# Attention and two MoE layers on one core: v, k and q laid out for their loads, and the second product of the dense MLP in tiles of 384 tokens, every second one accumulated in PSUM onto a copy by ScalarE

## The chip, the cores and the metric

The kernel runs on one core of a Trainium2 chip. The metric is the device time of one execution in microseconds (us); less is better. The engines are PE (TensorE, matrix products), DVE (VectorE), ACT (ScalarE), POOL (GpSimd) and SP (SyncE, which issues the DMAs). PE writes its products to PSUM, which has eight banks; DVE and ACT read them from there.

## The reference

Three layers, one after the other, all in float32:

```python
p_packed = sm_attn(p, k, v)          # 4 batches, 8 heads, 32 packed queries, 576 keys, head size 64
x = sm_attn(q, p_packed, p_packed)   # 576 queries per batch -> x is [2304, 512]
h = x @ w_in                         # [512, 2048]
x = (h * (1.0 / (1.0 + np.exp(-h)))) @ w_out          # [2048, 512]: the dense MLP
P = exp(logits - max); 8 rounds of row and column normalisation   # gate, 8 experts
out = sum over e of P[:, e] * (max(x @ w1[e], 0) @ w2[e])
```

## The kernel before

Every float32 product is made of three products of reduced parts: an operand is split into a part `h` (a cast by ACT) and the rest `l` (a subtraction by DVE), and hh, hl and lh are added up in PSUM.

**Attention and chunk 0.** The tokens are 4 batches of 576. Their steps are small nodes of a planner (`plan`), which is given costs (for example 1.68 us on SP for a load of k), priorities (`PR`) and an order of loads (`LOADS`), and writes out the order of every engine ahead of time. Loads come as k and q in pieces of [128, 2, 576], v in [128, 4, 256] and [64, 256], and weights of the dense MLP, which arrive as 64-bit floats and are converted in some steps on ACT and DVE (`ctin`, `ctout`, then `win`, or `woh` and `wol`). In a batch PE makes scores `s` in two halves, DVE transposes them (`e`), sums and divides, transposes back to `a2f`, splits into `a2h` and `a2l`. From these gemm1 starts.

**The dense MLP.** The 2048 hidden columns are four chunks `c` of 512. The work of a chunk is in units of one half batch (288 tokens): `u` (the input weights times the packed values, split as `U`, or `Uh` and `Ul`), gemm1 (`g` at L633, four tiles of 12 matmuls of 128x288), the gate function (`graw` at L663, on ACT), its split into `gT` (L664 on ACT, L665 on DVE), and gemm2 (`g` at L686: 4 tiles of 128 output columns, 12 matmuls of 288 each). In chunk 0 ACT copies the tile to `x2a` (batches 0 and 1) or `x2b` (2 and 3) (L691), in chunks 1 to 3 DVE adds it to that (L693). gemm2 of a unit is put behind gemm1 of the next. Chunk 0 is the planner's; chunks 1 to 3 are an order written out by hand, in which `pump` after each tile takes a share `RATE[c]` of a step of `pre`, the weight forms of the second MoE.

**The second MoE's weight forms.** Sums and differences `S` of weight blocks are made by DVE (L807); each is cast to `po` by ACT (L144), its rest follows by DVE (L145), and SP stores both to device memory (`w1d<-po`). The pool `po` has two buffers. In chunk 3, once `gh` is opened at batch `order[c][2]`, all remaining forms are taken this way.

**The second MoE.** A first expert runs in plain form (`u` L1002, `d` L1021) while the forms `xg` of x are made; then seven products of blocks (`X`, `Y`, `Z` at L1157; `d` at L1109), in which some tiles of PSUM are first filled by an ACT copy (L1105), added to by PE, and copied back (L1117).

Of the kernel before, what the change touches and what calls it, by code (L numbers as in the profile page):

```python
# [28 lines left out]
RATE = {1: 42 / 64, 2: 37 / 64, 3: 35 / 42}  # L29
CONV = 0.55  # L30
# [19 lines left out]
}  # L50

LOADS = "o0 i3 i0 k0 o2 k3 i2 v0 i1 q0 k1 v3 v1 o1 q3 o3 g v2 q1 q2 k2"
# [52 lines left out]
def fused_kernel(  # L105
# [24 lines left out]
    hp, hp_st = pool("hp", 4, side="left")  # L130
# [28 lines left out]
    class Plan:  # L159
# [13 lines left out]
        def order(self):  # L173
# [6 lines left out]
            while left:  # L180
# [46 lines left out]
                for c, k in t["give"]:  # L227
# [7 lines left out]
                 "a1T": 2, "ppm": 2, "ct": 4, "one": 1, "y": 4, "cr": 2, "cc": 2})  # L235
    kv, a2, u, gT = {}, {}, {}, {}
    win, wout = {}, {}
# [20 lines left out]
    def plan_loads():  # L258
        def kq(n, b, g):
            def fn():  # L260
                t = att.tile([128, 2, S], F32, tag="kq", bufs=8, name=f"{n}{b}{g}")
                src = kT if n == "k" else qT
                fixed(nc.sync.dma_start(t, src[b, 256 * g:256 * g + 256, :]
                                        .rearrange("(j p) s -> p j s", p=128)))
                kv[n, b, g] = t
            plan.add((n, b, g), "SP", 1.68, fn, take=[("kq", 1)])

        def vv(b, g):
            def fn():
# [236 lines left out]
    def conv2(c, kind, j):  # L506
# [9 lines left out]
        z = cvp["t2"].tile([128, 1024], F32, tag="ct2", name=f"ct{kind}{c}{j}")  # L516
# [58 lines left out]
    def plan_conv1(kind):  # L575
        for j in range(2):
# [5 lines left out]
            plan.add(g + (1,), "ACT", 2.35, nx, [g + (0,)], take=[("cc", 1)])  # L582
            plan.add(g + (2,), "DVE", 1.42, nx, [g + (1,)])
            plan.add(g + (3,), "DVE", 1.25, nx, [g + (2,)])
            done = [("cr", 1)] + [("cc", 1)] * (kind == "in")
            plan.add(g + (4,), "DVE", 1.25, nx, [g + (3,)], take=[("w", 1)] if kind == "in" else [], give=done)
            if kind == "out":
                plan.add(g + (5,), "ACT", 1.08, nx, [g + (4,)], take=[("w", 2)])
                plan.add(g + (6,), "DVE", 1.25, nx, [g + (5,)], give=[("cc", 1)])
# [47 lines left out]
    def gemm1_tile(c, b, half, f):  # L637
# [18 lines left out]
    def gemm1(c, b, half, pump):  # L656
        for j in range(WID[c] // 256):
# [6 lines left out]
            act.copy(out=t[:, 0], in_=raw)  # L664
            dve.tensor_tensor(t[:, 1], raw, t[:, 0].bitcast(F32), op=ALU.subtract)  # L665
            for i in range(2):
                gT[c, b, half, 2 * j + i] = t[:, :, i]
# [515 lines left out]
    def sinkhorn():  # L1183
        lgs = {}
        for hh in (1, 0):
# [8 lines left out]
            lg = const.tile([32 * nj, w], F32, name=f"lgs{hh}")  # L1194
# [63 lines left out]
    def close_att():  # L1258
# [36 lines left out]
    pre = pre_w1(list(range(G0)), 0)  # L1295
# [8 lines left out]
    def pump_conv(w):  # L1304
        due[1] += w * CONV
        if due[1] >= 1:
            due[1] -= 1
            cvn.step()

    with tc.manual_schedule(engines={mybir.EngineType.PE, mybir.EngineType.DVE, mybir.EngineType.Activation}):  # L1310
        for i, (c, b) in enumerate(seq):
# [14 lines left out]
            for half in range(2):  # L1326
                if c == NC - 1 and b == order[c][0] and half == 0:
                    box["ct_st"].close()
                    cv_st.close()
# [7 lines left out]
                if half == 1 and nxt is not None:  # L1337
# [3 lines left out]
                if pend is not None:  # L1341
# [159 lines left out]
```

## Time and profile before

| | |
|---|---|
| median of 3 runs (lowest to highest) | 1790.02 us (1788.94 to 1791.48) |
| the profiled execution | 1790.24 us |
| its span, first to last instruction | 1788.5 us |
| PE busy | 1768.5 us, 99% |
| DVE busy | 1454.3 us, 81% |
| ACT busy | 1040.2 us, 58% |

The span is 1.7 us shorter than the execution's time. Busy shares are means over the whole span, and stages differ; a matmul's own duration overlaps with the next one's, so that the pace of PE is read from a stretch of many. The table does not tell what PE waits for; the rows further below do.

### The profile page before, as it was taken

How to read it: one execution, taken by the hardware profiler on the slowest of the kernel's cores; microseconds unless marked ns; L12 is line 12 of the kernel's file. 1: busy time of each engine (PE TensorE's matmuls, PEld its weight loads, DVE VectorE, ACT ScalarE, POOL GpSimd, SP SyncE). 2: the span in 40 equal slices, each digit the busy share in tenths (PEclk: the TensorE clock that was granted, in tenths of full speed). 3: DMA queues.
4: the chain of work that ended last, by engine and by line, in shares of the span. 5: the costliest groups of instructions: out<-in, count | busy, mean ns of one | idle time of the engine just before them, and what ended most of it. 6: DMA issues, size and time to landing. Idle time of an engine off the chain costs nothing.

```text
span 1788.5 us, 25903 instructions
## 1 busy us (share of the span) xinstructions
PE 1768.5 (99%) x9852; PEld 1510.3 (84%) x9852; DVE 1454.3 (81%) x1972; ACT 1040.2 (58%) x1631; POOL 1.0 (0%) x8
## 2 busy tenths in 40 slices
PE   6999999999999999999999999999999999999998
PEld 4999999999998888888888888888888888888887
DVE  7868897658776998999888999887777777777778
ACT  6766655445454566666666666656555555555555
POOL 0000000000000000000000000000000000000000
PEclk9999999999999999999999999999999999999999
DMA  9425866865665655455554555965455444545442
GB/s 338 176 95 208 298 236 255 305 210 175 212 212 171 216 197 168 174 188 192 197 171 167 176 171 200 323 234 165 153 168 165 163 153 143 169 159 169 150 130 94
DMA packets 146619, 341.78 MB, mean 191 GB/s; under 512 B 11952, under 2 KB 53568, under 8 KB 145600
## 3 DMA queue, kind: packets, MB, share of 16 engines
q1 hardware_dynamic: 146496, 340.14, 56.3%
q8 instruction: 77, 1.26, 0.3%
q14 instruction: 46, 0.38, 0.1%
HBM read 256.66 MB, written 83.44 MB: 190 GB/s over the span
## 4 chain that ended last, share of the span: by engine, by line
PE 94%; DMA 3%; DVE 2%; ACT 1%; issue 0%; SPq 0%; DVEq 0%; ACTq 0%
PE d L1109 33%; PE X L1157 19%; PE g L686 10%; PE Z L1157 10%; PE u L1002 5%; PE g L633 5%; PE Y L1157 5%; PE d L1021 5%; DMA v<-in_v_dram 1%; PE u L247 1%; DMA w1d<-po 1%; DMA rawout<-in_moe_w_out_dram 0%; DMA rawin<-in_moe_w_in_dram 0%; PE s L247 0%; PE lg L1191 0%
## 5 line engine op out<-in xcount | busy, mean ns | idle before, releaser
L145 DVE TENSOR_TENSOR lo<-hb,hi 128x1024 fp32r<-128x1024 f32 x224 | 273.7, 1222 | 33.2 <-ACT hi L144 32.2
L1109 PE MATMUL d<-hi,w2f 128*128 128x512 f32 x896 | 294.2, 389 | 0.0
L1157 PE MATMUL X<-xf,w1l 128*128 128x512 f32 x1152 | 276.9, 389 | 0.0
L144 ACT CAST hi<-hb 128x1024 fp32r<-128x1024 f32 x224 | 235.3, 1051 | 64.9 <-PE d L1109 59.5
L1157 PEld LDWEIGHTS X<-xf,w1l 128*128 128x128 f32 x1152 | 216.2, 188 | 44.9
L1121 DVE TENSOR_TENSOR M<-d,M 128x512 f32<-128x512 f32 x204 | 140.4, 688 | 100.7 <-PE d L1109 100.7
L1117 ACT COPY M<-d 128x512 f32<-128x512 f32 x234 | 137.4, 589 | 143.2 <-PE d L1109 140.2
L686 PE MATMUL g<-gT,woh 128*128 128x288 f32 x1024 | 207.4, 297 | 0.0
L1109 PEld LDWEIGHTS d<-hi,w2f 128*128 128x128 f32 x896 | 168.1, 188 | 35.0
L1109 PE MATMUL d<-lo,w2f 128*128 128x512 f32 x448 | 174.3, 389 | 0.0
L686 PEld LDWEIGHTS g<-gT,woh 128*128 128x128 f32 x1024 | 163.7, 188 | 12.3 <-issue 4.7
L1109 PE MATMUL d<-hi,w2l 128*128 128x512 f32 x512 | 167.8, 389 | 0.0
L686 PE MATMUL g<-gT,wol 128*128 128x288 f32 x512 | 150.5, 294 | 0.0
L1105 ACT COPY d<-M 128x512 f32<-128x512 f32 x216 | 127.1, 589 | 20.7 <-DVE M L1121 19.3
L1109 PE MATMUL d<-hi,w2g 128*128 128x512 f32 x384 | 125.7, 389 | 0.0
L1109 PEld LDWEIGHTS d<-hi,w2l 128*128 128x128 f32 x512 | 96.1, 188 | 20.3 <-ACT d L1105 0.4
L1164 ACT COPY cp<-X 128x512 f32<-128x512 f32 x128 | 74.5, 583 | 46.5 <-PE X L1157 46.4
L1109 PE MATMUL d<-lo,w2l 128*128 128x512 f32 x256 | 99.6, 389 | 0.0
L1109 PEld LDWEIGHTS d<-lo,w2f 128*128 128x128 f32 x448 | 84.1, 188 | 17.5
L1157 PE MATMUL Y<-xf,w1f 128*128 128x512 f32 x384 | 97.3, 389 | 0.0
L686 PEld LDWEIGHTS g<-gT,wol 128*128 128x128 f32 x512 | 96.4, 188 | 0.0
L1002 PE MATMUL u<-xs,w1h 128*128 128x256 f32 x512 | 94.4, 285 | 0.0
(205 smaller groups left out, 3317.1 us busy)
## 6 DMA issues: line engine op xcount, KB each, us to landing
r<-in_moe_w_dram SPq DMA_DIRECT2D x128, 512.0 KB, 4.1
w1l<-w1d SPq DMA_DIRECT2D x128, 512.0 KB, 4.0
w1d<-po SPq DMA_DIRECT2D x64, 512.0 KB, 4.4
w2d<-w2f SPq DMA_DIRECT2D x64, 512.0 KB, 4.1
w2l<-w2d SPq DMA_DIRECT2D x64, 512.0 KB, 3.7
rb<-in_moe_w_dram SPq DMA_DIRECT2D x96, 256.0 KB, 2.7
sb<-in_moe_w_dram SPq DMA_DIRECT2D x48, 256.0 KB, 2.8
pb<-pd SPq DMA_DIRECT2D x16, 512.0 KB, 5.2
```

The source lines that it names most:

```text
L144: act.copy(out=hi, in_=raw)
L145: eng.tensor_tensor(out=lo, in0=raw, in1=hi.bitcast(F32), op=ALU.subtract)
L633: pe.matmul(ps, lhs[:, fs], rhs, start=(n == 0), stop=(n == 5))
L686: pe.matmul(ps[:, :HS], lhs, rhs, start=(n == 0), stop=(n == 3 * nf - 1))
L1002: pe.matmul(ps[:, i], w[:, k % 2, f], x[:, k], start=(n == 0), stop=(n == 11))
L1021: pe.matmul(ps, h[:, l, f % 2, 128 * tt:128 * tt + 128], w[:, f % 2], start=(fh == 0 and n == 0), stop=(fh == 1 and n == 11))
L1105: act.copy(out=ps, in_=m)
L1109: pe.matmul(ps, w[:, l, c, 128 * d:128 * d + 128], r[:, c], start=(n == 0 and not seed), stop=(n == 5), skip_group_check=seed)
L1117: act.copy(out=m, in_=ps)
L1121: dve.tensor_tensor(m, ps, m, op=ALU.add)
L1157: pe.matmul(ps, w[:, l, c, 128 * i:128 * i + 128], x[:, r, c], start=(n == 0 and p in (1, 7)), stop=(n == 5), skip_group_check=p in (2, 6, ...
L1164: act.copy(out=t, in_=ps)
```

## The change

The host lays v, k and q out so that each load is contiguous per partition: a row of k or q is 4608 B in place of two of 2304 B, one of v 4 KB in place of four of 1 KB. The planner has new priorities, a new order of loads and new costs for them; the batches are now taken in the order 0, 2, 1, 3 (before 0, 3, 1, 2). The split gate values go to two rings that hold four half batches, so that gemm2 in chunks 1 to 3 can take tiles of 384 tokens (`gemm2_wide`, L725). From the ninth tile on each tile with an even `d` is seeded: ACT copies the slice of x2 to PSUM one tile ahead (`seed`, L710), PE adds the 12 products to it, ACT copies it back (L730). Odd tiles are added by DVE as before (L732). The buffers `ct2` of the conversion go, the values are converted in place; the forms `xg` begin at step 8 in place of 9. In the changed kernel the lines have other numbers: graw and its cast are L672 and L673, po L145, u L251, gemm1 L641.

```diff
-RATE = {1: 42 / 64, 2: 37 / 64, 3: 35 / 42}
-CONV = 0.55
+RATE = {1: 46 / 64, 2: 38 / 64, 3: 36 / 53}
+CONV = 0.6
+TW = 384
...
-LOADS = "o0 i3 i0 k0 o2 k3 i2 v0 i1 q0 k1 v3 v1 o1 q3 o3 g v2 q1 q2 k2"
+LOADS = "i2 o3 k0 o2 i0 k2 i1 v0 i3 q0 k1 v2 v1 q2 o0 g o1 k3 q1 q3 v3"
...
-                fixed(nc.sync.dma_start(t, src[b, 256 * g:256 * g + 256, :]
-                                        .rearrange("(j p) s -> p j s", p=128)))
+                fixed(nc.sync.dma_start(t, src[b, g]))
...
-            plan.add((n, b, g), "SP", 1.68, fn, take=[("kq", 1)])
+            plan.add((n, b, g), "SP", 1.52, fn, take=[("kq", 1)])
...
-            t = hp.tile([128, 2, 2, HS], F32R, tag="h", name=f"gT{j}")
+            q = (b % 2) * S + half * HS
+            hi, lo = (ring[j].rearrange("p (f l) s -> p l f s", l=2)[:, l, :, q:q + HS] for l in range(2))
...
-    def gemm2(c, b, half, psp, tag, pump):
-        for d in range(4):
-            for _ in gemm2_tile(c, b, half, d, psp, tag):
-                pass
-            pump(1.6)
+    seeded, wides = {}, [0]
+
+    def seed(c, sb, t, d):
+        if d % 2 == 0 and wides[0] >= 8:
+            k = (c, sb, t, d)
+            wides[0] += 1
+            seeded[k] = box["p3"].tile([128, 512], F32, tag="y", name=f"g2w{c}{sb}{t}{d}")
+            act.copy(out=seeded[k][:, :TW], in_=x2[sb][d][:, TW * t:TW * t + TW])
+
+    def gemm2_wide(c, sb, t, d, ahead, pump):
+        ps = seeded.pop((c, sb, t, d), None)
+        on = ps is not None
+        if not on:
+            wides[0] += 1
+            ps = box["p3"].tile([128, 512], F32, tag="y", name=f"g2w{c}{sb}{t}{d}")
+        if ahead:
+            seed(*ahead)
+        ds, q = slice(128 * d, 128 * d + 128), slice(TW * t, TW * t + TW)
+        n = 0
+        for f in range(4):
+            hi, lo = wout[c, f // 2]
+            for lhs, rhs in ((hi, 0), (hi, 1), (lo, 0)):
+                pe.matmul(ps[:, :TW], lhs[:, f % 2, ds], ring[f // 2][:, 2 * (f % 2) + rhs, q],
+                          start=(n == 0 and not on), stop=(n == 11), skip_group_check=on)
+                n += 1
+        dst = x2[sb][d][:, q]
+        if on:
+            act.copy(out=dst, in_=ps[:, :TW])
+        else:
+            dve.tensor_tensor(dst, ps[:, :TW], dst, op=ALU.add)
+        pump(2 + 2 / 15)
...
+                if unit_:
+                    tiles += [(c, b // 2, unit_ - 1, d) for d in range(4)]
+                keep = {0: 2, 1: 2, 2: 2, 3: 4}[unit_]
...
+                while len(tiles) > keep:
+                    n = tiles.pop(0)
+                    gemm2_wide(*n, tiles[0] if tiles else None, pump)
...
-                if s >= 9 and slot:
+                if s >= 8 and slot:
                     next(xg, None)
```

**ACT in the third quarter of chunk 3.** The rows are ACT's own order; `g1_3010` is gemm1 of chunk 3, batch 0, second half, first pair of tiles, `g2w3122` is the wide tile of chunk 3, x2b, t = 2, d = 2, and po14 and po15 are weight forms. Before:

```order
L663 ACTIVATE graw_4281<-g1_3001_4267 128x576
L664 CAST gT1_4280<-graw_4281 128x576
L144 CAST po14_6_4299<-S14_2_4228 128x512
L144 CAST po14_7_4318<-S14_3_4259 128x512
L144 CAST po14_5_4337<-S14_1_4226 128x512
L144 CAST po14_3_4356<-S14_4_4261 128x512
L663 ACTIVATE graw_4379<-g1_3010_4365 128x576
L664 CAST gT0_4378<-graw_4379 128x576
L663 ACTIVATE graw_4397<-g1_3011_4383 128x576
```

And now:

```order
L730 COPY x2b0_1366<-g2w3120_3887 128x384
L145 CAST po14_6_3968<-S14_2_3884 128x512
L145 CAST po14_7_3973<-S14_3_3902 128x512
L710 COPY g2w3122_3979<-x2b2_1368 128x384
L145 CAST po14_5_3994<-S14_1_3882 128x512
L672 ACTIVATE graw_4012<-g1_3010_3999 128x576
L673 CAST ring0_103<-graw_4012 128x2x288
L145 CAST po14_3_4016<-S14_4_3904 128x512
L672 ACTIVATE graw_4034<-g1_3011_4021 128x576
L673 CAST ring1_1742<-graw_4034 128x2x288
```

Before, four po casts stood in one piece ahead of graw; now a copy back stands ahead of them, a seed between the second and the third, and graw of `g1_3010` between the third and the fourth.

**DVE where the first batch's attention ends.** The rows are DVE's order; `a2l0` is the lower part of batch 0, which gemm1 reads, `ctout` are steps of the conversion of an output weight, `e_2<-s2_20` is the transposition of the scores of batch 2. Before:

```order
L496 ISA ctout01_613<-rawout01_374,ctout01_613 128x1024
L455 TENSOR_TENSOR a2l0_622<-a2f0_564,a2h0_621 128x1152
L608 TENSOR_TENSOR U030_640<-u030_627,U030_640 128x512
L608 TENSOR_TENSOR U031_657<-u031_628,U031_657 128x512
L504 TENSOR_TENSOR wol00_181<-ctout01_613,woh00_180 128x512
L483 TENSOR_SCALAR ctout03_672<-ctout03_672 128x512
L484 TENSOR_SCALAR ctout03_672<-ctout03_672 128x512
L485 SCALAR_TENSOR_TENSOR ctout03_672<-rawout03_389,ctout03_672 128x512
L496 ISA ctout03_672<-rawout03_389,ctout03_672 128x1024
L397 STREAM_TRANSPOSE e_3_725<-s2_30_648 128x576
```

And now:

```order
L461 TENSOR_TENSOR a2l0_636<-a2f0_569,a2h0_635 128x1152
L489 TENSOR_SCALAR ctout00_642<-ctout00_642 128x512
L490 TENSOR_SCALAR ctout00_642<-ctout00_642 128x512
L491 SCALAR_TENSOR_TENSOR ctout00_642<-rawout00_374,ctout00_642 128x512
L502 ISA ctout00_642<-rawout00_374,ctout00_642 128x1024
L489 TENSOR_SCALAR ctout01_646<-ctout01_646 128x512
L490 TENSOR_SCALAR ctout01_646<-ctout01_646 128x512
L491 SCALAR_TENSOR_TENSOR ctout01_646<-rawout01_393,ctout01_646 128x512
L502 ISA ctout01_646<-rawout01_393,ctout01_646 128x1024
L510 TENSOR_TENSOR wol00_690<-ctout00_642,woh00_689 128x512
L403 STREAM_TRANSPOSE e_2_712<-s2_20_571 128x576
```

Before, one conversion of an output weight stood ahead of `a2l0` and one between it and the transposition; now both stand behind `a2l0` and ahead of the transposition.

## Rows read from the trace of the kernel before

**Rows 1.** The page's table of engines, and the clock in 40 slices.

```profile
PE 1768.5 (99%) x9852; PEld 1510.3 (84%) x9852; DVE 1454.3 (81%) x1972; ACT 1040.2 (58%) x1631; POOL 1.0 (0%) x8
...
PEclk9999999999999999999999999999999999999999
```

**Rows 2.** PE's waits: engine line, what for, total us, times, longest.

```profile
PE u L247 <- ACT graw L663: 0.8, 1, 0.8
PE d L1021 <- DVE w2l L145: 0.8, 1, 0.8
```

**Rows 3.** Windows: us, busy (instructions) of PE, PEld, DVE, ACT, POOL, PEclk, DMA share, GB/s.

```profile
24.00:26.60 2.60, 2.21 (x19) 1.09 (x16) 2.40 (x5) 2.12 (x8) 0.00 (x0) 1.00 1.05 391
29.90:33.60 3.70, 3.16 (x57) 2.18 (x56) 3.67 (x6) 1.95 (x4) 0.00 (x0) 1.00 1.11 315
...
144.20:375.00 230.80, 229.90 (x1794) 219.60 (x1792) 193.66 (x318) 124.64 (x191) 0.00 (x0) 1.00 0.75 271
```

**Rows 4.** The chain that ended last: start us, us, what.

```profile
249.90 6.40 PE g L686 x48
...
456.78 2.87 PE u L1002 x24
...
564.53 2.72 PE X L1157 x12
```

**Rows 5.** Groups by line, 144.2 to 375 us: shapes, count, busy us, mean ns.

```profile
L144 ACT CAST po<-S 128x512 fp32r<-128x512 f32 x63 | 36.1, 619 | 24.0 <-DMA w1d<-po 16.6 <-DVE S L807 7.3
L664 ACT CAST gT<-graw 128x576 fp32r<-128x576 f32 x44 | 29.7, 675 | 1.4
L663 ACT ACTIVATE graw<-g 128x576 f32<-128x576 f32 x44 | 28.6, 650 | 65.3 <-PE g L633 65.2
...
L145 DVE TENSOR_TENSOR po<-S,po 128x512 fp32r<-128x512 f32 x64 | 43.4, 684 | 9.7 <-ACT po L144 9.7
...
L693 DVE TENSOR_TENSOR x2b<-g,x2b 128x288 f32<-128x288 f32 x48 | 21.6, 452 | 3.7 <-PE g L686 3.5
```

**Rows 6.** The page's costliest groups: the copy that fills a PSUM tile.

```profile
L1105 ACT COPY d<-M 128x512 f32<-128x512 f32 x216 | 127.1, 589 | 20.7 <-DVE M L1121 19.3
```

**Rows 7.** Groups by line on ACT, 44 to 144 us.

```profile
L691 ACT COPY x2b<-g 128x288 f32<-128x288 f32 x16 | 6.0, 404 | 8.9 <-PE g L686 8.9
```

**Rows 8.** DVE's timeline, 26.5 to 52 us: start, us, instruction, idle before.

```profile
27.39 1.45 DVE L397 STREAM_TRANSPOSE e<-s 128x576 f32<-128x576 f32 x2 [0.51 <-PE s L247]
...
39.20 0.43 DVE L483 TENSOR_SCALAR ctout<-ctout 128x512 f32<-128x512 f32 x1 [0.24 <-ACT ctout L480]
...
41.56 1.35 DVE L455 TENSOR_TENSOR a2l<-a2f,a2h 128x1152 fp32r<-128x1152 f32 x1
42.83 1.28 DVE L608 TENSOR_TENSOR U<-u,U 128x512 fp32r<-128x512 f32 x2
```

**Rows 9.** PE's timeline, 40 to 53 us.

```profile
43.15 0.80 PE L633 MATMUL g<-a2h,U 128*128 128x288 f32 x4
...
50.66 1.25 PE L247 MATMUL u<-win,ppT 64*32 64x512 f32 x16
51.84 0.53 PE L686 MATMUL g<-gT,woh 128*128 128x288 f32 x2
```

**Rows 10.** ACT's timeline, 331 to 354 us.

```profile
332.83 1.13 ACT L144 CAST po<-S 128x512 fp32r<-128x512 f32 x2
339.44 0.62 ACT L144 CAST po<-S 128x512 fp32r<-128x512 f32 x1 [5.48 <-DMA w1d<-po]
...
353.61 0.62 ACT L144 CAST po<-S 128x512 fp32r<-128x512 f32 x1 [7.67 <-DMA w1d<-po]
```

**Rows 11.** The page's DMA issues: KB each, median us from issue to landing.

```profile
w1d<-po SPq DMA_DIRECT2D x64, 512.0 KB, 4.4
```

**Rows 12.** DVE's timeline, 552 to 560 us.

```profile
557.74 2.36 DVE L145 TENSOR_TENSOR w2l<-r,w2h 128x1024 fp32r<-128x1024 f32 x2
```

More of the change, by code (lines that the diff above doesn't have):

```diff
@@ L234, in fused_kernel @@
     plan = Plan({"p": 4, "s": 2, "kq": 8, "vt": 4, "w": 14, "x": 4, "h": 4, "g": 2, "a1": 2,
-                 "a1T": 2, "ppm": 2, "ct": 4, "one": 1, "y": 4, "cr": 2, "cc": 2})
+                 "a1T": 2, "ppm": 2, "ct": 4, "one": 1, "y": 4, "cr": 2})
     kv, a2, u, gT = {}, {}, {}, {}
+    ring = [hp.tile([128, 4, 2 * S], F32R, tag="h0", name="ring0")]
+    kq4 = hp.tile([128, 4, 2, S], F32, tag="h1", name="kq4")
+    kqn = []
     win, wout = {}, {}
@@ L515, in conv2 @@
         low, high = words[:, :, 0], words[:, :, 1]
-        z = cvp["t2"].tile([128, 1024], F32, tag="ct2", name=f"ct{kind}{c}{j}")
+        if kind == "in":
+            win[c, j] = unit([128, 2, w], F32, f"win{c}{j}")
+            z = win[c, j].rearrange("p k f -> p (k f)")
+        else:
+            z = unit([128, 1024], F32, f"ct{c}{j}")
         zi = z.bitcast(U32)
@@ L581, in plan_conv1 @@
             plan.add(g + (0,), "SP", 3.0, nx, ["close"], take=[("cr", 1)])
[L582 removed]
+            plan.add(g + (1,), "ACT", 2.35, nx, [g + (0,)], take=[("w", 1)])
             plan.add(g + (2,), "DVE", 1.42, nx, [g + (1,)])
             plan.add(g + (3,), "DVE", 1.25, nx, [g + (2,)])
[L585 to L586 removed]
+            plan.add(g + (4,), "DVE", 1.25, nx, [g + (3,)], give=[("cr", 1)])
             if kind == "out":
                 plan.add(g + (5,), "ACT", 1.08, nx, [g + (4,)], take=[("w", 2)])
[L589 removed]
+                plan.add(g + (6,), "DVE", 1.25, nx, [g + (5,)], give=[("w", 1)])
     up_ps = {}
@@ L643, in gemm1_tile @@
             gpair[k] = gt.tile([128, 2, HS], F32, tag="graw", name="graw")
-            hpair[k] = hp.tile([128, 2, 2, HS], F32R, tag="h", name=f"gT{f}")
-        raw, t = gpair[k], hpair[k]
+            hpair[k] = ring[0][:, len(hpair) % 4].rearrange("p (i l s) -> p i l s", i=2, l=2)
+        raw, t = gpair[k], hpair[k].rearrange("p i l s -> p l i s")
         act.activation(raw[:, i], ps[:, :HS], AF.Silu)
@@ L660, in gemm1 @@
                 gemm1_mm(ps[:, i, :HS], c, b, half, 2 * j + i)
-            t = hp.tile([128, 2, 2, HS], F32R, tag="h", name=f"gT{j}")
+            q = (b % 2) * S + half * HS
+            hi, lo = (ring[j].rearrange("p (f l) s -> p l f s", l=2)[:, l, :, q:q + HS] for l in range(2))
             raw = gt.tile([128, 2, HS], F32, tag="graw", name="graw")
             act.activation(raw, ps[:, :, :HS], AF.Silu)
[L664 to L667, printed above, removed]
+            act.copy(out=hi, in_=raw)
+            dve.tensor_tensor(lo, raw, hi.bitcast(F32), op=ALU.subtract)
             pump(0.8)
@@ L1265, in close_att @@
             open_(name, n, keep=name in ("S", "r1"))
+        box["pre"] = pre_w1(list(range(G0)), 0)
+        next(box["pre"])
         cvp["p2"], box["cv_st"] = pool("cv2", 2, side="right", reuse_waits="tile")
-        cvp["t2"], box["ct_st"] = pool("ct2", 2, side="right", reuse_waits="tile")
         cv1.update({(1, kind, j): conv2(1, kind, j) for kind in ("in", "out") for j in range(2)})
@@ L1294, in fused_kernel @@
     cvn = None
-    pre = pre_w1(list(range(G0)), 0)
+    pre = box["pre"]
+    next(pre)
+    next(pre)
     due = [0.0, 0.0]
@@ L1308, in pump_conv @@
             cvn.step()
+    tiles = []
+    ring.append(hp.tile([128, 4, 2 * S], F32R, tag="h1", name="ring1"))
     with tc.manual_schedule(engines={mybir.EngineType.PE, mybir.EngineType.DVE, mybir.EngineType.Activation}):
@@ L1336, in fused_kernel @@
                 gemm1(c, b, half, pump)
-                if half == 1 and nxt is not None:
+                if nxt is not None and half == ((c, b) != seq[NC][:2]):
                     if nxt[0] != c:
@@ L1340, in fused_kernel @@
                     make_u(*nxt)
-                if pend is not None:
-                    gemm2(*pend, *psp, pump)
-                    if pend == (NC - 1, order[c][2], 0):
+                if unit_:
+                    tiles += [(c, b // 2, unit_ - 1, d) for d in range(4)]
+                keep = {0: 2, 1: 2, 2: 2, 3: 4}[unit_]
+                if (c, b) == seq[NC][:2]:
+                    keep = len(tiles)
+                if nxt is None and half == 1:
+                    keep = 0
+                while len(tiles) > keep:
+                    n = tiles.pop(0)
+                    gemm2_wide(*n, tiles[0] if tiles else None, pump)
+                    if n == (NC - 1, order[c][2] // 2, 0, 3):
                         for _ in pre:
@@ L1346, in fused_kernel @@
                         cvn = Rot([pre0()], 1)
-                pend = (c, b, half)
-        gemm2(*pend, *psp, pump)
         cvn.drain()
```

32 lines of the change are left out of this document (18 added, 14 removed), and 26 rows, old and new, of the table PR.

## The prediction

> **What bounds the kernel now.** I read the table of engines first. TensorE (PE) is busy for 1768.5 of 1788.5 us, 99%, and its granted clock stays in the top tenth in all 40 slices [rows 1]; in the stretches asked for it is 1.00, the upper of the two levels, 2.4 GHz [rows 3]. VectorE (DVE) and ScalarE (ACT) have slack as a share. So the time is what PE has to do, plus its waits. The second view is PE's waits: after the first loads the longest are under 1 us [rows 2]. Third, the chain: dense stretches whose pace can be read [rows 4]. From 43.15 us, when PE starts the first g1 product [rows 9], the kernel is one long row of matmuls; only fewer or cheaper matmuls, an earlier start, or a stall in the row can change the time. I price the four in that order.
>
> **1. Wide tiles.** The chain shows 48 matmuls of 288 columns in 6.40 us, 24 of 256 in 2.87 and 12 of 512 in 2.72 [rows 4]: 133.3, 119.6 and 226.7 ns each. Columns at 2.4 GHz make 120, 106.7 and 213.3 ns, so each pays 13 ns more whatever its width, and one of 384 should take 160 + 13.3 = 173.3 ns. In chunks 1 to 3 gemm2 was 96 tiles of 12 matmuls, 1152 x 133.3 = 153.6 us; it becomes 72 tiles of 12, 864 x 173.3 = 149.7 us. The columns are the same; 288 fixed costs go: **-3.8 us**. It cannot be lower than nothing, since the columns don't grow.
>
> The Trainium skill ("TensorE: Matmul & The Clock Gate", section "Back-to-back issue gap") speaks for less: an isolated warm matmul follows the one before after N/2.4 + 2.5 ns. By that rule the edit would bring 288 x 2.5 = 0.7 us, and the time would be 3.1 us above mine. The traced 13 ns at three widths disagree, and the measurement decides.
>
> **2. Seeds in place of adds.** 96 DVE adds at 452 ns (43 us) [rows 5] become 40 at a width of 384; 32 tiles instead take two ACT copies each, one onto PSUM before and one back. ACT took 404 ns for 288 columns [rows 7] and 589 for 512, with PSUM on the out side [rows 6], so 0.48 us for 384 by a line through the two, and 64 x 0.48 = 31 us more on an engine that is busy 124.6 of 230.8 us there [rows 3]: 67%. On average that lies beside PE, for a tile lasts 12 x 0.173 = 2.08 us and the seed is issued a tile ahead. ACT works in order, though. Behind a 1.05 us conversion cast with one copy of 0.48 on each side it takes 2.0 of a 2.08 us tile. I put **+0.4** for a few such meetings; below this nothing, above it rival B. Starting a product on a seeded bank is no new operation: the second MoE does it [rows 6].
>
> **3. The start.** k and q, in packets of 2304 B, come at 391 GB/s; with v, in packets of 1 KB, the rate is 315 [rows 3]. A half batch of v is 589,824 B: 1.87 us at 315, 1.51 at 391. I take 391 for all new packets, all of which are larger; -0.36 each. Ahead of q of batch 0 stand, now as before, six halves of weights, two batches of k and one of v: 0.7 us earlier. That q gates the first transposition of e (27.39 us, released by PE's s) [rows 8], which then starts at 26.65. From there DVE's row leads to a2l, 27.39 to 42.91 us = 15.5 us, which releases the first g1. In the new order the out conversion of 2.6 us (39.20 with its wait, to 41.56) stands behind a2l, and two more subtractions U (1.28 the pair) [rows 8] ahead of it: 15.5 - 2.6 + 1.3 = 14.2, and I allow 0.6 for waits on ACT that the conversion covered. a2l is done at about 41.5 instead of 42.9: -1.4 if that were all. What is late next: two out conversions (2.36 each) and a wol subtraction now stand between a2l and the transpositions of batches 2 and 1, which free the two score buffers that PE's s for batch 1 needs. By 41.5 + 4.7 + 0.7 + 0.8 + 0.7 + 0.7 + 0.8 + 0.7 and the last 0.8, less 0.07 of overlap a step, the last transposition ends near 50.9 and PE's s after it at 51.5. The first g2 can start at 51.6, against 51.84 before [rows 9], but before the 16 matmuls of u for the next half (50.66 to 51.84) were done by then, and now they are still to come: -0.2 + 1.2 = **+0.9**. Bounds: -2 (the early a2l is kept, and no allowance) to +2.5 (the allowance again, and one more hand-over of 1 us).
>
> **4. Casts that wait for a store.** In chunk 3 from the third quarter on, all weight forms go through two po buffers. Each is written by ACT (0.62) and DVE (0.68) [rows 5] and stored by w1d<-po, 4.4 us from issue to landing [rows 11]. ACT casts po14_6 and _7 at 332.83, then stands until 339.44 for a buffer [rows 10]; graw is behind it in the row, and the u product needs the bank that graw frees: 0.8 us of PE stall [rows 2]. In the second such set ACT waits 7.67 us [rows 10], and no PE wait stands for it: half a unit of finished gT lay in between. In the new order the same casts stand behind the copy of g2w3120 back and around a seed, and gemm2 is nearer to its gemm1. From the end of 3120 PE has tile 3121 (2.08) and two g1 (1.60 each) before u31: 5.3 us. ACT has copy 0.48, cast and subtraction 1.3, 0.3 of hand-overs, landing 4.4 = 6.5, then the third cast 0.62 and graw 0.65 = 7.75. Stall 2.4 where it was 0.8: **+1.6**. In the second set PE has from the end of tile 3000 one tile, two g1 and two tiles = 9.4 us before tile 3010; ACT has 6.5 + 2 casts + 2 x (graw 0.65, ring 0.67) = 10.4, then copy back and seed 0.96 = 11.3: **+1.8**. Lower bound of each: none, if the S forms come earlier and the stores run shorter; upper: by the traced waits of 6.6 and 7.7 us in place of my 4.4 of landing, about 1 us more each.
>
> **5. The rest.** The x forms of the first expert's end are begun a step earlier (s from 8). Before, the last w2l subtractions run at 557.74 behind them [rows 12] and PE waits 0.8 us for w2l [rows 2]; a step earlier that goes, with what the pace loses: **-1.0** (nothing to -1.3). Small waits of tiles in chunk 2 go: -0.2. The ct buffers and the gate's result tile move between pools; I cost them at nothing: conversions in chunks 1 and 2 run on DVE and ACT ahead of need, and if that cover were gone one costs a g1 its wait of about 1.2 us.
>
> Sum: -3.8 + 0.4 + 0.9 + 3.4 - 1.0 - 0.2 = -0.3 on the profiled execution's 1790.24, which is 0.22 above the median. **Forecast 1789.7 us.**
>
> **The rivals.**
> - **A, the casts don't bite.** If the stores land soon enough, the +3.4 is nothing and the old 0.8 goes too: -0.3 - 3.4 - 0.8 = -4.5, so 1785.5; with the start also at its lower bound 1782.6. For it: the second set cost PE nothing before though ACT waited 7.67 us. Against: the new row puts PE closer behind ACT, and the landing times are those of a busy DMA (0.75 of the time, 271 GB/s) [rows 3]. Chance 0.28.
> - **B, ACT's row becomes the bound: slower.** graw and its cast (0.65 and 0.68) come twice a unit and each must be out before the next seed; if every one of the 32 seeds comes 0.25 us late, +8 us: 1797.7. It decides once the seed and copy back (0.96) with what stands between them exceed the 2.08 us of the odd tile. For: ACT at 67%, and the po waits above leave ACT standing. Against: four PSUM banks and a tile's lead. Chance 0.11.
> - **C, the fixed cost per matmul doesn't fall with their number**, because it is a tile's or a weight load's: then only part 1 is lost, 1789.7 + 3.1 = 1792.8 where a small part stays. The three widths in rows 4 speak against it. Chance 0.05. (The gap rule of the Trainium skill, "TensorE: Matmul & The Clock Gate", section "Back-to-back issue gap", gives this same time.)
>
> **How the numbers follow.** Forecast 0.53, A 0.28, B 0.11, C 0.05, others 0.03, half of them on each side. About 0.2%, 3.6 us, is what a measurement here can tell from no change. Faster than 1786.4 is A and a little of the forecast's own lower bounds: 0.30; slower than 1793.6 is B, and the forecast with both po bounds and the start's upper one: 0.15; the rest 0.55. The range leaves out B and the far end of A: 1784.0 to 1794.0; the forecast's own is 1787 to 1793.
>
> **What would show it.** Right: 12 wide matmuls in 2.08 us in the chain; gemm2 of chunks 1 to 3 at 149.7 us; first g1 at about 41.75 and a gap between the last g1 and the first g2 that eats it; PE waits of 2.4 and 1.8 us with graw, ring or seed as releaser near the third quarter of chunk 3; no wait for w2l at the end of the first expert. Wrong: many short PE waits on a seed or a copy back (B); no wait over 0.5 us there (A); wide tiles of 2.2 us (C); and the start, if k or v land later than computed, since every us of it stands in the sum at full price.

## The result, and the profile after

The changed kernel takes 1800.03 us (median of 6; 1799.05 to 1800.87) against 1790.41 for the kernel before, run beside it: a ratio of 1.0054 (95% interval 1.0041 to 1.0067), 9.6 us slower. The forecast was 1789.7, in a range from 1784.0 to 1794.0. The profiled execution has 1800.11 us and a span of 1798.3, 9.9 more than before.

The table of engines first, to be read against [rows 1]: PE is busy for 1.9 us more, though it has 292 matmuls fewer.

```profile
PE 1770.4 (98%) x9560; PEld 1510.3 (84%) x9560; DVE 1439.5 (80%) x1916; ACT 1065.3 (59%) x1695; POOL 1.0 (0%) x8
```

Where is the time lost? Four marks on PE's timeline split the span: the first g1, the gate's first product, the first u of the first expert, the first X. From the start to the first g1 it is 43.15 us before and 41.67 after (-1.5). From there to the gate it is 331.96 before and 342.77 after (**+10.8**). The gate takes the same time. The first expert takes 184.82 and 185.61 (+0.8), and the rest, from X to the end, is 0.2 shorter. The sum is +9.9; the loss lies in the dense MLP.

The chain there shows that the wide tiles themselves run as costed: 48 matmuls of 384 columns in 8.32 us, 173.3 ns each (start us, us, what).

```profile
190.77 8.32 PE g2w L725 x48
```

PE's waits (total us, times, longest) show what is new against [rows 2]: seeds, Ul, and the wait for w2l larger than before, not gone.

```profile
PE g2w L725 <- ACT g2w L710: 6.1, 2, 3.0
...
PE g L641 <- DVE Ul L627: 1.5, 2, 1.4
...
PE d L1054 <- DVE w2l L146: 1.1, 1, 1.1
...
PE u L251 <- ACT graw L672: 0.8, 1, 0.8
PE g L641 <- ACT graw L672: 0.7, 1, 0.7
```

**The wait near 180 us.** PE's timeline (start, us, instruction, idle before); then ACT's and DVE's in the same place.

```profile
178.17 0.34 PE L725 MATMUL g2w<-ring,wol 128*128 128x384 f32 x1
181.55 0.62 PE L725 MATMUL g2w<-ring,woh 128*128 128x384 f32 x2 [3.04 <-ACT g2w L710]
...
183.32 0.84 PE L725 MATMUL g2w<-ring,woh 128*128 128x384 f32 x2
```

```profile
176.46 0.48 ACT L730 COPY x2a<-g2w 128x384 f32<-128x384 f32 x1 [1.05 <-PE g2w L725]
180.07 1.04 ACT L544 CAST woh<-ct 128x1024 fp32r<-128x1024 f32 x1 [3.13 <-DVE ct L539]
181.02 0.48 ACT L710 COPY g2w<-x2b 128x384 f32<-128x384 f32 x1
```

```profile
177.01 1.22 DVE L534 SCALAR_TENSOR_TENSOR ct<-rawout,ct 128x1024 uint32<-128x1024 uint32 x1
178.15 0.75 DVE L674 TENSOR_TENSOR ring<-graw,ring 128x576 fp32r<-128x576 f32 x1
178.81 1.22 DVE L539 CUSTOM_DVE_ANT_0 ct<-rawout,ct 128x2048 uint16<-128x2048 uint16 x1
```

Read backwards in time: PE waits for the seed, which ACT starts at 181.02. ACT stood idle from 176.9 to 180.07, because the next instruction in its row was the woh cast, and that needs a result that DVE gives only at 180.0, at the end of a dense row. The seed itself needs nothing that is late: in e5_lead2, below, it runs at 175.2, ahead of the cast. And from 183.32 on PE's matmuls start 320 ns apart in place of 173: the clock fell behind the wait.

**The wait near 360 us** has the same form with a store in DVE's place. ACT's timeline, to be read against [rows 10]:

```profile
350.68 0.49 ACT L710 COPY g2w<-x2a 128x384 f32<-128x384 f32 x1
357.15 0.62 ACT L145 CAST po<-S 128x512 fp32r<-128x512 f32 x1 [5.99 <-DMA w1d<-po]
357.68 0.65 ACT L672 ACTIVATE graw<-g 128x576 f32<-128x576 f32 x1
...
360.70 0.47 ACT L730 COPY x2a<-g2w 128x384 f32<-128x384 f32 x1
361.07 0.49 ACT L710 COPY g2w<-x2a 128x384 f32<-128x384 f32 x1
```

The third po cast stands for 5.99 us; graw, ring, copy back and the seed of tile 3010 follow it, and PE starts that tile at 361.62 after 3.01 us of idle time. The windows show the granted clock of the two places (us; busy of PE, PEld, DVE, ACT, POOL; clock; DMA share, GB/s); it is 1.00 in all windows of that length between 194 and 354 us.

```profile
184.00:194.00 10.00, 10.00 (x58) 10.00 (x57) 7.76 (x12) 7.76 (x13) 0.00 (x0) 0.88 0.87 336
...
354.00:364.00 10.00, 6.99 (x35) 6.67 (x34) 3.28 (x5) 4.34 (x8) 0.00 (x0) 0.83 0.61 246
364.00:374.00 10.00, 10.00 (x56) 10.00 (x56) 2.91 (x7) 4.35 (x11) 0.00 (x0) 0.83 0.01 2
```

A mean of 0.88 or 0.83 is a part of the window at 1.2 GHz: 10 matmuls behind the first wait and 16 behind the second start 320 ns apart in place of 173, 1.5 and 2.4 us more.

The stretch from the first g1 to the gate can be accounted for by the distances between the starts of PE's matmuls (a wait read so is up to 0.2 us longer than the idle time in the views). The two seed waits make 3.2 and 3.2, with 0.3 behind the second, the half clock (1.2 GHz) 1.5 and 2.4, Ul 1.5 and 0.3, graw 0.9 at 135 us and 0.8 at 341. The last was there before too. So 13.3 us are new; the width gives 3.8 back; 1.3 us is spread over gaps under 0.25. That makes the 10.8.

### The profile page after: what moved, and what is told of

Same layout as the page of the kernel before. It is cut to its first block, busy times and chain, and to the rows that moved or that the text cites. A ratio compares the mean times of both kernels' runs of the same rounds, so it can differ in the third digit from the quotient of the medians.

```text
span 1798.3 us, 25343 instructions
## 1 busy us (share of the span) xinstructions
PE 1770.4 (98%) x9560; PEld 1510.3 (84%) x9560; DVE 1439.5 (80%) x1916; ACT 1065.3 (59%) x1695; POOL 1.0 (0%) x8
## 4 chain that ended last, share of the span: by engine, by line
PE 92%; DMA 3%; DVE 3%; ACT 2%; issue 1%; SPq 0%; DVEq 0%; ACTq 0%
PE d L1142 33%; PE X L1190 19%; PE Z L1190 10%; PE g2w L725 7%; PE Y L1190 5%; PE g L641 5%; PE u L1035 5%; PE d L1054 4%; PE g L693 3%; DMA v<-in_v_dram 1%; DMA w1d<-po 1%; PE u L251 1%; DMA kq<-in_qT_dram 0%; DVE po L146 0%; DVE S L840 0%
## 5 line engine op out<-in xcount | busy, mean ns | idle before, releaser
L145 ACT CAST hi<-hb 128x1024 fp32r<-128x1024 f32 x224 | 235.2, 1051 | 65.3 <-PE d L1142 59.3
L725 PE MATMUL g2w<-ring,woh 128*128 128x384 f32 x576 | 151.3, 344 | 6.1 <-ACT g2w L710 6.1
L725 PEld LDWEIGHTS g2w<-ring,woh 128*128 128x128 f32 x576 | 105.6, 193 | 15.7 <-issue 7.5
L725 PE MATMUL g2w<-ring,wol 128*128 128x384 f32 x288 | 98.2, 341 | 0.0
L145 ACT CAST w1f<-rb 128x512 fp32r<-128x512 f32 x96 | 59.8, 624 | 56.5 <-PE d L1142 40.7
```

Source lines behind the costliest of these rows:

```text
L145: act.copy(out=hi, in_=raw)
L725: pe.matmul(ps[:, :TW], lhs[:, f % 2, ds], ring[f // 2][:, 2 * (f % 2) + rhs, q], start=(n == 0 and not on), stop=(n == 11), skip_group_ch ...
```

## The experiments

In the text the profiled stretch from the first g1 to the gate's first product is "the stretch" (before: 331.96 us, the change: 342.77). It leaves out the start, which is read at the end of this part. The kernel before had 1790.4 to 1791.1 us beside these runs. How far can one profile be trusted? Two of the kernels below, e6_po3 and e10_po3_s9, have the same order of instructions up to the gate on PE, DVE, ACT and in the loads and stores, and their stretches are 335.49 and 337.89 us: a difference of 2.4 us between two profiles is not yet an effect.

**1. The change taken apart: no seeds; tiles of 288; seeds earlier; a third po buffer.** e1_no_seed:

```diff
-        if d % 2 == 0 and wides[0] >= 8:
+        if d % 2 == 0 and wides[0] >= 999:
```

> The changed kernel with all 72 wide tiles added by DVE, none seeded (32 x 2 ACT copies go, 32 DVE adds come). Theory Q, the seeds wait in ACT's in-order row behind instructions that themselves wait (a woh cast for DVE, a po cast for a store): the PE wait of 3.0 us at 178 us and the half clock after it (1.6 us) go, the wait at 358 us shrinks from 3.0 to about 1.5, since graw of the same unit still stands behind the po cast: 1800.0 - 4.8 - 1.5 to 4 = 1791.2 to 1793.7. Rival D, the late worker is DVE: 32 adds more at 0.55 us make DVE later, waits on Ul and ct grow: 1800 or slower, with PE waits on DVE in place of those on seeds.

Measured 1796.32 us, 3.7 less than the change, where 6 to 9 were expected; ratio to before 1.0031 (1.0019 to 1.0043). The stretch has 339.42. Both seed waits are gone, but PE now waits 1.7 us for the ring (DVE) at 192 to 195 us and 3.2 for Ul, with half clock behind the waits for the ring and behind the longest one for Ul, 2.1 us. Neither theory holds alone.

e3_narrow: TW is 288, no seeds, and a unit's four tiles are kept until the next gemm1:

```diff
-TW = 384
+TW = 288
...
-                if unit_:
-                    tiles += [(c, b // 2, unit_ - 1, d) for d in range(4)]
-                keep = {0: 2, 1: 2, 2: 2, 3: 4}[unit_]
-                if (c, b) == seq[NC][:2]:
-                    keep = len(tiles)
+                tiles += [(c, b // 2, unit_, d) for d in range(4)]
+                keep = 4
...
-        pump(2 + 2 / 15)
+        pump(1.6)
```

> The changed kernel with tiles of 288 tokens in gemm2 of chunks 1 to 3, one unit behind gemm1 as in the kernel before, none seeded: layout, loads, priorities, rates and rings stay. If a matmul's fixed cost is 13 ns: 3.8 us slower than the run without seeds, apart from waits. If the fixed cost doesn't fall with their number: 0 to 0.7 us slower. Theory Q: no wait on a seed, as none is there, and the wait at the end of chunk 3 is gone because gemm2 is a unit behind gemm1: about 1793 to 1795. Rival P, the new plan and rates are what costs: near 1800, with waits at the same places.

Measured 1793.85; 1.0018 (1.0009 to 1.0027). The stretch has 336.25: the old tiles with the new plan lose 4.3 us there. gemm2 takes 154.7 us with 133 ns from matmul to matmul, as before the change. The largest wait is 2.7 us for graw, with half clock behind it, and ACT's row tells why:

```profile
177.63 1.04 ACT L544 CAST woh<-ct 128x1024 fp32r<-128x1024 f32 x1 [5.32 <-DVE ct L539]
178.96 0.62 ACT L145 CAST po<-S 128x512 fp32r<-128x512 f32 x1 [0.28 <-DVE S L840]
179.49 0.64 ACT L672 ACTIVATE graw<-g 128x576 f32<-128x576 f32 x1
```

The same cast waits for the same DVE step; here graw stands behind it in place of a seed. So at this place the seed is only what happened to be there. The wait of a cast does not cost PE time by itself, though. The kernel before has a like one, with graw right behind it, and PE has no wait there:

```profile
196.56 1.05 ACT L535 CAST woh<-ctout 128x1024 fp32r<-128x1024 f32 x1 [4.99 <-DVE ctout L530]
197.51 0.65 ACT L663 ACTIVATE graw<-g 128x576 f32<-128x576 f32 x1
```

e5_lead2 passes two tiles ahead:

```diff
-                    gemm2_wide(*n, tiles[0] if tiles else None, pump)
+                    gemm2_wide(*n, [m for m in tiles[:2] if m[3] % 2 == 0 and m not in seeded], pump)
...
-        if ahead:
-            seed(*ahead)
+        for m in ahead:
+            seed(*m)
```

> The changed kernel with each seed issued two tiles ahead in place of one. Theory Q: the seed of 178 us then stands ahead of the woh cast that waits for DVE, so the 3.0 us wait and the half clock behind it go, 4.8 us; the wait at 358 us stays, because that seed still stands behind the po cast: 1795.2. Rival D (DVE is late, the wait only moves on to the next reader of the converted weights or to Ul): 1799 to 1800.

Measured 1799.09; 1.0047 (1.0034 to 1.0059). At 178 us PE no longer waits, and at 357 us it does (3.3), both as theory Q has it; but the time comes back at the next readers, ring, graw and Ul, as D has it:

```profile
PE g2w L725 <- ACT g2w L710: 3.3, 1, 3.3
PE u L251 <- ACT graw L672: 2.1, 2, 1.1
...
PE g L641 <- DVE Ul L627: 1.8, 3, 1.2
PE g2w L725 <- DVE ring L674: 1.8, 2, 1.1
```

e6_po3 gives the forms a third buffer when gh is open:

```diff
+                    open_("pq", 1)
...
-            t = st["po"].tile([128, 2, 2, 256], F32R, tag="po", name=f"po{s}_{p}")
+            n = "pq" if p == 7 and "gh" in st else "po"
+            t = st[n].tile([128, 2, 2, 256], F32R, tag=n, name=f"po{s}_{p}")
```

> The changed kernel with a third buffer for the po forms in the second half of chunk 3, so that the third cast of a set doesn't wait for the store of the first. Theory Q: the waits at 358 us (3.2 and 0.3, with 2.4 of half clock behind) and at 340 us (0.9) go: 1800.0 - 6.8 = 1793.2. Rival (the row ahead of that seed is late for its copies and casts themselves, not for the store): 0 to -1 us, 1799 to 1800.

Measured 1794.83; 1.0021 (1.0012 to 1.0030): 5.2 us off the median, and 7.3 off the stretch (335.49), with no PE wait over 0.25 us from 252 us to the gate. Of the 7.3 us, 6.8 lie behind 335 us, where the buffer acts. That the store held up ACT's row in chunk 3 is shown. The other 0.5 us says something of the half clock: the order ahead of chunk 3 is that of the change, and PE waits 3.0 us for the same seed, but the clock does not fall behind it. PE then waits 1.0 us more for graw and Ul, so that most of the 1.5 us of half clock in the change had only taken the place of these waits. The runs below stand on this kernel.

**2. What is late in chunk 1?** e7_po3_rates takes the old rates:

```diff
-RATE = {1: 46 / 64, 2: 38 / 64, 3: 36 / 53}
-CONV = 0.6
+RATE = {1: 42 / 64, 2: 37 / 64, 3: 41 / 53}
+CONV = 0.55
```

> The run with the third po buffer (1794.8), and with the rates of the kernel before for the weight forms and conversions in chunks 1 and 2 (42/64, 37/64, conversions 0.55; chunk 3 at 41/53 to take the rest). In ACT's row the woh cast then stands behind the seed of the first x2b tile, not ahead of it. Theory R, the new rates bunch the DVE work and put casts that wait for DVE ahead of seeds: the waits at 180 us (3.2) and on Ul near 250 us (1.5) and 205 us (1.1) go, 5.8 us: 1789 to 1791. Theory Q alone (only the place of the seed): -3.2, 1791.6, Ul waits stay. Rival (the rates don't matter, DVE is late anyway): 1794 to 1796.

Measured 1797.80; 1.0039 (1.0025 to 1.0053): slower than e6_po3 and above all three expectations. The 3.2 us at 180 are gone, but PE waits 5.8 us for five seeds at other places. The rates of before are no cure by themselves.

e8_po3_yield adds two empty steps ahead of the woh cast (`if c > 1: yield; yield`), so that DVE has more time for what the cast reads.

> The run with the third po buffer, and two empty steps ahead of the woh cast of chunks 2 and 3, so that DVE's part of the conversion has two tiles more of time; rates as in the change. Theory Q: the seed wait at 180 us (3.2) goes: 1791.6; the waits on Ul (1.9 in all) stay, since DVE's row has as much ahead of Ul as before. Rival (DVE is late by more than two tiles, or the seed waits for something else): 1794 to 1796.

Measured 1793.47; 1.0017 (1.0008 to 1.0026). The median is 1.4 less, but the stretch of its profile, 336.59, is 1.1 longer than that of e6_po3, so a gain isn't shown. The wait at 180 is gone; at 191 us a seed makes PE wait 2.5 behind a po cast that itself waits 1.77 for DVE's S, and Ul costs 2.8.

e9_po3_no_seed, e6_po3 without seeds (the edit of e1_no_seed):

> The run with the third po buffer, and all wide tiles added by DVE. From the run without seeds alone (1796.3) the rest of the wait at the end of chunk 3 and the 1.1 us on graw at 345 us should go: about 1794.5 to 1795, no better than with seeds, because in chunk 1 waits on ring and Ul (DVE) take the place of the seed wait. If seeds as such cost time apart from that one wait: 1792 or less.

Measured 1795.16; 1.0028 (1.0017 to 1.0039), about as expected and no faster than with seeds: waits on the ring (1.9) and Ul (4.0) take the seeds' place.

e10_po3_s9 puts the x forms back to `s >= 9`:

> The run with the third po buffer, and the x forms begun at step 9 as before. If the earlier start lengthens the first expert (185.6 us in the changed kernel's trace from its first u to X, 184.8 before): -0.8 us there, 1794.0. If its wait for w2l (1.1 us) comes from elsewhere: the same, 1794.8. If the early start brought what I put on it: +1.0, 1795.8.

Measured 1794.29; 1.0021 (1.0012 to 1.0030). The medians differ by 0.5, too little to tell; in the profiles the first expert takes 184.82 us, as before, and 185.59 in e6_po3. Of the other kernels, the two with step 9 have 184.8 and all with step 8 have 185.6 or 185.7, so the earlier start costs 0.8 us, where I had put a gain of 1.0. In the dense MLP, with the same order, PE waits 1.4 us for a seed near 359 us here, which it doesn't in the profile of e6_po3.

**3. Is it the lead?** Another theory (L): gemm2 now follows its gemm1, and gemm1 its u, by two tiles (4.2 us) at some units, where it was four of 1.6 us. The edit is the same in all four, `keep = 4` in place of `keep = {0: 2, 1: 2, 2: 2, 3: 4}[unit_]`, on the change, on e6_po3, on e9_po3_no_seed and on e8_po3_yield.

> The changed kernel with four tiles of gemm2 always left over when a unit's tiles are taken, in place of two (four after the last): after each u product PE then has four wide tiles (8.3 us) before the gemm1 that reads Ul, where it had two (4.2 us) at every second unit; gemm2 reads a ring at least four tiles after its gemm1 (before the change: four of 1.6 = 6.4 us). Theory L, the lost lead: the waits on Ul (1.5 us at 248) go, those on seeds shrink where the seed follows two tiles after a late row; the po wait at 358 us goes at least in part, since tile 3010 comes four tiles later: 1792 to 1795. Rival Q (only the seeds' place behind waiting casts counts): the wait of 3 us stays at a woh cast and at a po cast, 1798 to 1800.

> The same with the third po buffer (1794.8 without the longer lead). Theory L: Ul waits (1.9 us) go, the seed wait at 180 us goes if its row has caught up: 1789.5 to 1793. Rival Q: 1794 to 1795.

> The same with the third po buffer and no seeds (1795.2 without the longer lead). Theory L: the waits on Ul (4.0 us) and on the ring (1.9 us), with the half clock near 196 and 254 us, go: 1789 to 1790.5, so that only the 1.0 us on graw at 135 us and the 0.6 longer first expert are left against the 3.8 us that the width gives. Rival D (DVE simply has too much to do in chunk 1): 1794 or slower.

> Third po buffer, longer lead, seeds, and two empty steps ahead of the woh casts (1793.5 without the longer lead). Theories L and Q together: no PE wait over 0.5 us between 140 and 375 us: 1787.5 to 1790. If one of them is still wrong: 1791 to 1793.

Measured 1802.16 (1.0062; 1.0049 to 1.0074), 1797.14 (1.0038; 1.0026 to 1.0051), 1797.84 (1.0040; 1.0026 to 1.0054) and 1794.86 (1.0025; 1.0017 to 1.0034): each slower than the run it stands on. All Ul waits are gone, which L had right, but in the second run six seeds wait instead:

```profile
PE g2w L725 <- ACT g2w L710: 6.3, 6, 1.6
```

And in the third PE waits 5.7 us for graw, which stands behind a po cast and a woh cast that both wait for DVE:

```profile
194.53 0.62 ACT L145 CAST po<-S 128x512 fp32r<-128x512 f32 x1 [5.56 <-DVE S L840]
197.33 1.04 ACT L544 CAST woh<-ct 128x1024 fp32r<-128x1024 f32 x1 [2.19 <-DVE ct L539]
```

A longer lead moves the waits within ACT's row and doesn't take them away; L falls as the main cause.

**4. DVE's load in chunk 1.** The rates become

```diff
-RATE = {1: 46 / 64, 2: 38 / 64, 3: 36 / 53}
+RATE = {1: 34 / 64, 2: 42 / 64, 3: 40 / 53}
```

on e6_po3, e9_po3_no_seed, e8_po3_yield, and on e6_po3 with the tiles of e3_narrow.

> The run with the third po buffer (1794.8), and a quarter fewer weight forms in chunk 1 (34/64 of a step in place of 46/64; chunks 2 and 3 at 42/64 and 40/53 take them), some 9 us of DVE less there. Theory D, DVE's row is dense in chunk 1 and whatever waits behind it (casts, seeds, Ul) comes late: the waits of 3.2, 0.5, 0.6 and 1.5 us between 178 and 250 us shrink to 1 to 2 in all: 1790 to 1791.5. Rival Q (only the place of a seed in ACT's row counts): it depends on where the casts now fall, 1793 to 1796.

> The same without seeds (1795.2 at the old rate). Theory D: 7.5 us of waits on DVE's ring and Ul and on graw go, with 1 us of half clock or so: 1787 to 1790. Rival (the shorter lead of gemm2 behind gemm1 is the cause, not DVE's load): waits on the ring and Ul of 4 us or more stay, 1792 to 1795.

> Third po buffer, seeds, two empty steps ahead of the woh casts (1793.5), and the lower rate in chunk 1. Theories D and Q: 1788.5 to 1790.5. If neither: 1793.

> Third po buffer, lower rate in chunk 1, tiles of 288 tokens as before the change, no seeds. It holds what layout, loads and plan give: the stretch from the first g1 to the gate's product should be that of the kernel before (332.0 us) plus the 0.9 us wait on graw at 135 us and what is left on Ul, 333 to 334, and the time 1790 to 1791.5. If the width gives 3.8 us, the run without seeds at the same rate is faster by that, less its waits.

Measured 1793.41 (1.0015; 1.0006 to 1.0024), 1791.61 (1.0006; 0.9997 to 1.0014), 1792.18 (1.0008; 0.9999 to 1.0017) and 1796.11 (1.0029; 1.0018 to 1.0041). The windows of chunk 1 in e9_po3_no_seed and then e16_po3_no_seed_slow1 (columns as above; the third busy time is DVE's):

```profile
144.20:217.00 72.80, 68.33 (x448) 63.96 (x447) 66.45 (x100) 41.34 (x61) 0.00 (x0) 1.00 0.83 294
```

```profile
144.20:217.00 72.80, 72.27 (x492) 68.03 (x491) 61.43 (x91) 42.05 (x61) 0.00 (x0) 1.00 0.69 253
```

DVE has 5 us less, and PE is busy 3.9 us more in the same 72.8 us: of its waits there (5.2 us) 0.7 is left. With seeds the waits of chunk 1 fall from 4.5 to 2.5. This is as D has it. But load alone isn't the cause, for the kernel before has as much of it in the same window, and PE waits 0.2 us there:

```profile
144.20:217.00 72.80, 72.67 (x567) 69.52 (x566) 66.43 (x106) 42.63 (x62) 0.00 (x0) 1.00 0.80 288
```

So the new plan has a part in these waits beside the load. And the forms moved on to chunk 2, where PE now waits:

```profile
PE u L251 <- ACT graw L672: 2.2, 1, 2.2
...
PE g L641 <- DVE Ul L627: 1.5, 2, 1.0
```

And the narrow one is 4.6 us above what was expected: PE waits 1.9 for Ul at 269 us and 2.3 for graw at 361, places where e3_narrow had little or nothing. That graw stands behind a po cast that waits for a store, in spite of the third buffer:

```profile
362.70 0.62 ACT L145 CAST po<-S 128x512 fp32r<-128x512 f32 x1 [4.89 <-DMA w1d<-po]
```

Two last kernels, e19_best without seeds and e20_best_seed with them, stand on e17_po3_yield_slow1 and move forms on from chunk 2 to 3 (rates 34/64, 36/64, 44/53) and the x forms to step 9.

> Third po buffer, no seeds, two empty steps ahead of the woh casts, x forms from step 9, rates 34/64, 36/64 and 44/53 (fewer weight forms in chunks 1 and 2, more in chunk 3). From the run without seeds at the lower rate (1791.6): its wait of 2.3 us on graw at 238 us, in chunk 2, came with the higher rate of chunk 2 and should go, with 0.5 of the first expert: 1788.5 to 1789.5, under the kernel before. If waits just move on to the next dense place: 1791 to 1792.

> The same with seeds (1792.2 at rates 34/64 and 42/64 with the x forms from step 8). Theory D: 1790 to 1791, seeds cost no more than DVE adds once DVE's row is light. Theory Q: some seeds still stand behind casts that wait, 1 to 2 us above the run without seeds.

Measured 1793.34 (1.0012; 1.0003 to 1.0022) and 1796.15 (1.0028; 1.0016 to 1.0039), both above what was expected. The wait for graw at 238 us went from 2.2 to 1.5 only, so it was not the rate of chunk 2 alone, and in chunk 3 new ones came: 2.0 in all near 356 us without seeds, and 2.6 at 357 on a seed with them. ACT's row shows another neighbour at each place. Ahead of graw at 238 us stands a step of the conversion that waits for the load of its weights, and in chunk 3, which now takes more forms, a po cast waits for a store again (two rows of e19_best, then one of e20_best_seed):

```profile
237.81 1.15 ACT L528 ACTIVATE ct<-rawout 128x1024 f32<-128x1024 f32 x1 [5.05 <-DMA rawout<-in_moe_w_out_dram]
...
353.87 0.62 ACT L145 CAST po<-S 128x512 fp32r<-128x512 f32 x1 [7.21 <-DMA w1d<-po]
```

```profile
354.97 0.62 ACT L145 CAST po<-S 128x512 fp32r<-128x512 f32 x1 [5.45 <-DMA w1d<-po]
```

**The start.** The order up to the first g1 is the same in the change and in these runs, yet their profiles have it at 41.67, 43.69, 41.93, 43.67, 42.96 and so on, between 41.59 and 43.69. The two ends, PE's timeline in the changed kernel and in e1_no_seed, each with the first g1 and the first g2:

```profile
41.67 0.77 PE L641 MATMUL g<-a2h,U 128*128 128x288 f32 x4
...
49.80 0.53 PE L693 MATMUL g<-ring,woh 128*128 128x288 f32 x2
```

```profile
43.69 0.77 PE L641 MATMUL g<-a2h,U 128*128 128x288 f32 x4
...
51.84 0.53 PE L693 MATMUL g<-ring,woh 128*128 128x288 f32 x2
```

Before, one profile has 43.15 [rows 9]. The loads did become faster: up to its first g1 the changed kernel moves 15.23 MB in 4913 packets at 366 GB/s, where the kernel before moved 14.60 MB in 8828 packets at 338. The scatter goes with their rate: in the first 41.5 us it is 365 GB/s in the change and 354 in e1_no_seed. But a scatter of 2.1 us covers what the layout does for the first g1; it stays open whether it does anything.

## Why the prediction was wrong, step by step

- **Wide tiles, -3.8: right.** A matmul takes 173.3 ns, as worked out. In e16_po3_no_seed_slow1, where no wait lies in gemm2, the 864 take 151.3 us from start to start, and the 1152 before took 154.8: 3.5 less. Rival C falls. The Trainium skill ("TensorE: Matmul & The Clock Gate", section "Back-to-back issue gap") gives N/2.4 + 2.5 ns for an isolated matmul, by which, as an estimate, one of 384 would take 162.5; the matmuls in this trace don't agree with it at this width either.
- **Seeds, +0.4: this is the step that failed.** I priced a meeting with a conversion cast by the cast's own 1.05 us and found that it fits into a tile. The cast waits for DVE first, 3.13 us, and in ACT's order the seed waits with it. In the view of [rows 5], in a row that I left out, the four woh casts of the kernel before have 9.5 us of idle time ahead of them (0.55, 4.99 and 4.00 us, and none ahead of one):

```profile
L535 ACT CAST woh<-ctout 128x1024 fp32r<-128x1024 f32 x4 | 4.2, 1050 | 9.5 <-DVE ctout L530 9.5
```

  I took the busy time from that row and not the idle time. Measured were 3.2 us of wait and 1.5 of half clock at 180 us, 4.7 in place of 0.4, and not 32 small waits; so rival B had the sign and the place (ACT's row) but not the mechanism it named, 0.25 us at each seed. What failed is the price of what stands ahead in the row, not that of the two copies: e9_po3_no_seed, without them, is no faster than e6_po3.
- **Casts that wait for a store, +1.6 and +1.8 (its own numbers make 1.9): mechanism right, sizes off.** The first wait stayed at 0.8, as it was before; the second, which I put on tile 3010, where it came, makes 3.2 and 0.3 with 2.4 of half clock: 5.9. With one buffer more e6_po3 takes 6.8 us off chunk 3. That a wait of 3 us can be followed by a time at 1.2 GHz was in no term of the sum; nothing in the trace of before showed such a wait after 43 us.
- **The start, +0.9: wrong.** I had the first g1 at about 41.75 and the first g2 at 51.6, with a gap between them that eats what the loads give. There is no such gap: the g2 comes 8.1 us after the g1 in the change, in e1_no_seed and in e6_po3, where before it came 8.7 after. That the first g1 came at 41.67 is luck, and so is a first g2 at 51.8 in some profiles: both scatter by some 2 us with the loads.
- **The rest, -1.2: wrong.** The wait for w2l is 1.1 us, not gone, and the first expert is 0.8 longer (e10_po3_s9). I had costed the conversions of chunks 1 and 2 at nothing, as work that runs ahead of need, and put "one costs a g1 its wait of about 1.2 us" if that cover were gone. It was gone: PE waits for Ul 1.4 us up to 249.88, and in DVE's row a step of a conversion and two of S stand ahead of Ul:

```profile
246.14 1.22 DVE L534 SCALAR_TENSOR_TENSOR ct<-rawout,ct 128x1024 uint32<-128x1024 uint32 x1
247.27 0.69 DVE L840 TENSOR_TENSOR S<-r,r 128x512 f32<-128x512 f32 x1
247.99 0.69 DVE L840 TENSOR_TENSOR S<-S,r 128x512 f32<-128x512 f32 x1
248.60 1.22 DVE L627 TENSOR_TENSOR Ul<-u,Uh 128x1024 fp32r<-128x1024 f32 x1
```

  This is the error of the seeds again. The 0.9 us on graw at 135 us stood in no term.

Added up over the span, in us: width -3.8, the seed at 180 us 4.7, the stores 5.9, Ul 1.8, graw at 135 us 0.9, small gaps 1.3, the first expert 0.8, the start -1.5, the end -0.2. That is +9.9, where the forecast had -0.3.

What the runs show of the cause: in ACT's row stand casts whose input DVE or a store gives late, and behind them, by turns, seeds, graw and ring, on which PE waits. The po store is settled at the rates of the change; with more forms in chunk 3 casts wait for it again (e18, e19, e20). In chunk 1, less DVE load takes the waits of the form without seeds from 5.2 to 0.7 us, though the kernel before bore the same load. Not settled is what of the plan makes e3_narrow lose 4.3 us and which order would be free of such waits: old rates, later casts, more lead and lower rates each took away waits at one place and brought some at another. What a seed costs by itself also stays open: with seeds less without, the medians differ by +3.7 (the change and e1), +1.8 (e15, e16), +2.8 (e20, e19), -0.3 (e6, e9) and -0.7 us (e12, e13), and the last two are within the noise. The best forms, e16_po3_no_seed_slow1 and e17_po3_yield_slow1, tie with the kernel before; none beats it.

## What to carry to other kernels

Work put into the row of an engine that takes its instructions in order is to be priced by the waits of what stands ahead of it, not by busy times: read the idle column of each group that it will follow, and set it against how long the reader can do without. In the kernel before a cast waited 5.0 us with graw behind it and cost PE nothing; in e3_narrow one of 5.3 us cost 2.7. A saving on the bound engine that also shortens the lead of its producers has to be weighed against the waits that the lead had hidden; here 3.8 us of matmuls were bought with 13 us of waits and slow clock. And to a wait on PE of 2 to 3 us add a chance of a slower clock behind it.

## What the hardware showed that was not expected

Behind waits of 3.2 us at 178 and 358 us 10 and 16 of PE's matmuls started 320 ns apart in place of 173, and the windows' granted clock fell to 0.88 and 0.83. It is not the wait's length alone: in e6_po3 a wait of the same length at 180 us was followed by matmuls 173 ns apart. Of the 16 waits of 2 us or more in the dense MLP of all traces here, 12 had a fall of the granted clock to 0.5 in or behind them, one of them a wait of 2.0 us (e7_po3_rates), and four had none (e6, e8, e9, e16). Two shorter waits close together, of 0.5 and 1.0 us, had one in e19_best; two of 1.3 and 0.7 in e9_po3_no_seed had none.

The time of the first g1 scatters by 2.1 us between profiles of the same start, and the stretch behind it by 2.4 us between two profiles of the same order.
